# Attention values times the first matrix: from four matmuls with zero blocks to eight without, on one core

## The chip, the cores and the metric

The kernel runs on one core of one Trainium2 chip. The metric is device time in microseconds (us) of one launch, the median of several runs. Engines are named as in the profile: PE (TensorE) with its weight loads (PEld), DVE (VectorE), ACT (ScalarE), POOL (GpSimd), SP (SyncE, which issues the DMAs).

## What is computed

```python
def sm_attn(qq, kk, vv):                       # softmax attention, scale 1/8
    s = scale * np.matmul(qq, kk.transpose(0, 1, 3, 2))
    a = np.exp(s - np.max(s, axis=-1, keepdims=True))
    return np.matmul(a / (np.sum(a, axis=-1, keepdims=True) + 1e-09), vv)

# q, k, v: 4 batches x 8 heads x 576 x 64; p: 4 x 8 x 32 x 64
p_packed = sm_attn(p, k, v)                    # 32 rows of 64 per head
out = sm_attn(q, p_packed, p_packed)
x = out.transpose(0, 2, 1, 3).reshape(2304, 512)

h = x @ w_in                                   # first layers, d_ff 2048
x = (h * np.clip(h + 3.0, 0.0, 6.0) / 6.0) @ w_out

P = routing(x @ w_gate)                        # exp, then 8 rounds of row and column scaling
for e in range(8):                             # second layers, 8 experts, 1024 wide
    out += P[:, e:e + 1] * (np.maximum(x @ w1[e], 0.0) @ w2[e])
```

All inputs are float32 but the weights of the first layers, `w_in` and `w_out`, which come as 64-bit floats and are decoded on the chip.

## The kernel before, in words

Nothing is emitted in the order of the source. The functions put operations, each with an engine, an estimated cost, the tiles it reads and writes (`reads`, `writes`, `fills`, `takes`) and a priority, into an `Order`; `Order.run` then plays a list scheduler: again and again it takes the operation that can start first by its estimates (ties by priority), gives it buffers, and emits it. So each engine's order is fixed before the launch, and a changed cost or a changed use of a buffer lays out the following work anew. `place` says how many buffers a tag has. PSUM tiles `ph` and `po` have two banks each to begin with and two more each from `second_phase` on, which comes when the attention is finished.

*Attention* (L494, eight units `u`, two per batch `b`; unit `j` of a batch has heads 4j to 4j + 3). A unit loads k, p (in units 0 and 1 only: `p_sb[0]` for unit 0 and `p_sb[1]` for the seven others, L519), q and v, in this order on SP. GpSimd copies a unit's 128 rows of `p` (4 heads x 32) twice side by side (`pd`, L543); a transpose and a mask (`maskb`, L574 to L584) make of it, for each of two pairs of heads `g`, a 128 x 64 block matrix `pt`. The scores and the values of the packed rows follow, and a second mask (`maskz`, L692) lays them out so that after a transpose `ppT[:, g, :]` (L708) is 128 x 64: rows are head in the pair (h) times 64, columns head times 32, and the two blocks off the diagonal are zero. The scores of the queries use it as a whole (L740). The results `ax` of the attention (`a2`) have 128 rows, 4 heads x 32, per unit.

*packed_weights* (L830). Since `out` of a head is a 576 x 32 matrix times the 32 x 64 packed values, the values are multiplied into the first matrix first: for a batch and a group of 256 columns of `w_in`, `pw` = values times `w1`, two units j of 128 rows x 256. That is four matmuls per group (L841), for j and g: 128 rows (h times 64) x 64 columns, 256 columns moving, all of a group into one `ph` bank of 128 x 512, j being the half of the bank. ACT then copies the bank to the high part `pwh`, rounded (L857), and DVE writes the rest into `pwl` (L862), both 512 wide. For the first six units of work (`TOGETHER`) a call has one group, after that two.

*layer1a, layer2a* (L878, L913). A block of 384 tokens goes through two groups at a time: four times layer 1 from `pw` and `ax` in three float32r products (L890 to L892) into a `ph` bank, which ACT (L903) and DVE (L908) read; then four times layer 2 with 12 matmuls each (L928 to L930) into a `po` bank, added to `acc` by DVE (L943).

*After that* the gate (L1115: four matmuls of 128 rows x 32 columns, each on its own 32 columns of the array), the routing, and the second layers (`layer1b`, L996 to L998, and `layer2b`, L1055 to L1057), which take three quarters of the time.

The tiles of the early stage, `hs`, `tmp` and the raw weights (`raw`, L392; decoding `m` and `m_early`, L348 to L373) are shared by all this.

## Time and profile before

| | us |
|---|---|
| median of 3 runs | 1955.41 |
| fastest and slowest run | 1952.35, 1956.96 |
| span of the profiled execution | 1952.2 |
| PE busy in it | 1915.1 (98%) |
| DVE busy | 1210.0 (62%) |
| ACT busy | 970.2 (50%) |
| POOL busy | 947.5 (49%) |

Engine names and lines (L841 is line 841 of the kernel) are those of the listing above. "out<-in" names the tile written and the tiles read. A float32 matmul shows as two records, a float32r matmul as one. The records of PE overlap, since a matmul is still draining when the next one starts; what a series of them costs is therefore read from the start of the first to the start of what comes next. The chain of work that ended last is followed back from the last instruction, at each step to what released it.

### The profile page before, as it was taken

How to read it: one execution, taken by the hardware profiler on the slowest of the kernel's cores; microseconds unless marked ns; L12 is line 12 of the kernel's file. 1: busy time of each engine (PE TensorE's matmuls, PEld its weight loads, DVE VectorE, ACT ScalarE, POOL GpSimd, SP SyncE). 2: the span in 40 equal slices, each digit the busy share in tenths (PEclk: the TensorE clock that was granted, in tenths of full speed). 3: DMA queues.
4: the chain of work that ended last, by engine and by line, in shares of the span. 5: the costliest groups of instructions: out<-in, count | busy, mean ns of one | idle time of the engine just before them, and what ended most of it. 6: DMA issues, size and time to landing. Idle time of an engine off the chain costs nothing.

```text
span 1952.2 us, 28194 instructions
## 1 busy us (share of the span) xinstructions
PE 1915.1 (98%) x10573; PEld 1735.2 (89%) x10573; DVE 1210.0 (62%) x1998; ACT 970.2 (50%) x2135; POOL 947.5 (49%) x987
## 2 busy tenths in 40 slices
PE   6999999999999999999999999999999999999998
PEld 4789999998899999999899999999999999999997
DVE  6996686447866676666755555555555555555554
ACT  6885674335455555555544443344444344443432
POOL 2444675236665666655634544435344343444431
PEclk9999999999999999999999999999999999999999
DMA  9931121001222222222310101111110111101102
GB/s 215 188 90 33 54 66 44 11 1 44 65 65 66 75 65 70 71 65 65 87 33 33 44 22 44 33 33 33 33 44 30 36 33 33 44 22 44 33 11 66
DMA packets 103546, 104.87 MB, mean 54 GB/s; under 512 B 42736, under 2 KB 78576, under 8 KB 103408
## 3 DMA queue, kind: packets, MB, share of 16 engines
q1 hardware_dynamic: 103408, 103.06, 19.4%
q8 instruction: 83, 1.36, 0.3%
q14 instruction: 55, 0.45, 0.1%
HBM read 98.32 MB, written 4.72 MB: 53 GB/s over the span
## 4 chain that ended last, share of the span: by engine, by line
PE 91%; DVE 5%; ACT 2%; DMA 1%; issue 1%; SPq 0%; POOL 0%; DVEq 0%; POOLq 0%; ACTq 0%
PE po L1055 13%; PE po L1056 13%; PE po L1057 13%; PE ph L996 12%; PE ph L998 12%; PE ph L997 12%; PE po L928 3%; PE po L930 3%; PE po L929 3%; PE ph L890 2%; PE ph L892 1%; PE ph L891 1%; PE ph L841 1%; DMA raw<-in_moe_w_out_dram 1%; DVE tmp L908 0%
## 5 line engine op out<-in xcount | busy, mean ns | idle before, releaser
L1079 DVE SCALAR_TENSOR_TENSOR acc<-po,Pr,acc 128x512 f32<-128x512 f32 x504 | 377.3, 750 | 287.2 <-PE po L1057 284.1
L433 POOL TENSOR_TENSOR hsl<-tmp,hsh 128x384 fp32r<-128x384 f32 x382 | 391.8, 1031 | 325.4 <-ACT hsh L428 272.4
L1055 PE MATMUL po<-w2h,hsh 128*128 128x512 f32 x1152 | 449.0, 390 | 0.0
L1056 PE MATMUL po<-w2l,hsh 128*128 128x512 f32 x1152 | 448.8, 390 | 0.0
L1057 PE MATMUL po<-w2h,hsl 128*128 128x512 f32 x1152 | 448.6, 389 | 0.0
L433 POOL TENSOR_TENSOR w1xl<-m,w1xh 128x256 fp32r<-128x256 f32 x152 | 111.5, 758 | 321.8 <-ACT w1xh L428 321.8
L1057 PEld LDWEIGHTS po<-w2h,hsl 128*128 128x128 f32 x1152 | 216.2, 188 | 45.3
L304 ACT ACTIVATE tmp<-ph 128x384 f32<-128x384 f32 x241 | 117.7, 489 | 274.8 <-PE ph L998 263.1
L1055 PEld LDWEIGHTS po<-w2h,hsh 128*128 128x128 f32 x1152 | 216.3, 188 | 41.8 <-DVE acc L1079 0.2
L1056 PEld LDWEIGHTS po<-w2l,hsh 128*128 128x128 f32 x1152 | 216.3, 188 | 41.5
L428 ACT ACTIVATE hsh<-tmp 128x384 fp32r<-128x384 f32 x480 | 242.4, 520 | 20.4 <-DVE tmp L908 12.6
L1010 DVE TENSOR_TENSOR tmp<-ph,tmp 128x384 f32<-128x384 f32 x288 | 159.8, 556 | 149.3 <-PE ph L998 129.7
L428 ACT ACTIVATE w2h<-raw 128x1024 fp32r<-128x1024 f32 x64 | 67.9, 1061 | 350.1 <-PE po L1057 338.1
L1018 ACT ACTIVATE tmp<-tmp 128x384 f32<-128x384 f32 x288 | 149.6, 520 | 87.2 <-DVE tmp L1010 82.8
L996 PE MATMUL ph<-ax,w1h 128*128 128x384 f32 x448 | 151.5, 338 | 3.3 <-DVE tmp L1010 3.3
L998 PE MATMUL ph<-ax,w1l 128*128 128x384 f32 x448 | 150.7, 336 | 0.0
L997 PE MATMUL ph<-ax,w1h 128*128 128x384 f32 x448 | 150.7, 336 | 0.0
L433 DVE TENSOR_TENSOR hsl<-tmp,hsh 128x384 fp32r<-128x384 f32 x98 | 105.6, 1078 | 42.0 <-ACT hsh L428 39.8
L433 POOL TENSOR_TENSOR w1l<-raw,w1h 128x512 fp32r<-128x512 f32 (+1 forms) x104 | 116.3, 1132 | 7.5 <-ACT w1h L428 6.8
L996 PE MATMUL ph<-xyh,w1h 128*128 128x384 f32 x320 | 108.3, 339 | 3.6 <-ACT tmp L304 3.6
L455 POOL TENSOR_TENSOR m<-raw 128x256 f32<-128x256 f32 x58 | 44.5, 770 | 138.7 <-DMA raw<-in_moe_w_dram 136.0
L998 PE MATMUL ph<-xyh,w1l 128*128 128x384 f32 x320 | 108.1, 338 | 0.0
(207 smaller groups left out, 4040.4 us busy)
## 6 DMA issues: line engine op xcount, KB each, us to landing
raw<-in_moe_w_dram SPq DMA_DIRECT2D x128, 512.0 KB, 3.5
raw<-in_moe_w_in_dram SPq DMA_DIRECT2D x16, 512.0 KB, 3.9
raw<-in_moe_w_out_dram SPq DMA_DIRECT2D x16, 512.0 KB, 3.6
k<-in_k_dram SPq DMA_DIRECT2D x32, 144.0 KB, 5.9
q<-in_q_dram SPq DMA_DIRECT2D x32, 144.0 KB, 4.5
v<-in_v_dram SPq DMA_DIRECT2D x8, 576.0 KB, 6.5
out_dram<-acc SPq DMA_DIRECT2D x36, 128.0 KB, 2.3
p<-in_p_dram SPq DMA_DIRECT2D x1, 224.0 KB, 5.7
```

The lines of the kernel that those rows point to most:

```text
L304: ("ACT", t_act(n, True), lambda: nc.scalar.activation(dst(), src(), AF.Copy)),
L428: t_act(n), lambda: nc.scalar.activation(dst(w.t[0]), src(), AF.Copy),
L433: lambda e: e.tensor_tensor(dst(w.t[1]), src(), as_f32(dst(w.t[0])), ALU.subtract),
L996: nc.tensor.matmul(out, wh[:, at + c, :], bh[:, c, :], start=first and c == 0, **on)
L997: nc.tensor.matmul(out, wh[:, at + c, :], bl[:, c, :], start=False, **on)
L998: nc.tensor.matmul(out, wl[:, at + c, :], bh[:, c, :], start=False, **on)
L1010: t_dve(n), lambda: nc.vector.tensor_tensor(u.t, ps.t[:, :n], u.t, ALU.add),
L1018: t_act(n, bool(ps)), lambda: nc.scalar.activation(c.t, src(), AF.Relu),
L1055: nc.tensor.matmul(ps.t, hh[:, f, ts], wh[:, f, :], start=(f == 0), stop=False)
L1056: nc.tensor.matmul(ps.t, hh[:, f, ts], wl[:, f, :], start=False, stop=False)
L1057: nc.tensor.matmul(ps.t, hl[:, f, ts], wh[:, f, :], start=False, stop=(f == NFC - 1))
L1079: lambda row=row, share=share, ps=ps: nc.vector.scalar_tensor_tensor(row(), ps.t, share(), row(), ALU.mult, ALU.add),
```

## The change

Each group's product of values and first matrix is split in two again, by head: the zero blocks of `ppT` are no longer multiplied. A matmul takes 64 rows (one head's 64) and the 32 columns of that head. To give the two units of a batch different places in the array, the heads of each second unit are swapped in pairs: unit j = 1 has its heads in the order 1, 0, 3, 2 within each 32-row block, in `p` (loaded in four pieces), in both masks (three blocks wide, of which a unit takes two, from j on) and so in all that follows. A call writes two `ph` banks, one for each j, with the groups side by side in each; ACT and DVE take them out in pieces of 256.

```diff
-        if u < 2:
-            of = slice(0, 1) if u == 0 else slice(1, NU)
+        if u in (0, 2):
+            of = slice(0, 1) if u == 0 else slice(1, B)
             dma(
                 64 * (of.stop - of.start),
                 lambda: nc.sync.dma_start(
-                    p_sb[u].t, p.rearrange("b (j h) n d -> (h n) (b j) d", j=2)[:, of, :]
+                    p_sb[u].t, p.rearrange("b (j h) n d -> (h n) j b d", j=2)[:, 0, of, :]
                 ),
                 writes=[p_sb[u]], **kw,
             )
+        if u == 1:
+            for x in range(4):
+                dma(
+                    32,
+                    lambda x=x: nc.sync.dma_start(
+                        p_sb[u].t[32 * x:32 * x + 32],
+                        p[:, 4 + (x ^ 1)].rearrange("b n d -> n b d"),
+                    ),
+                    fills=[p_sb[u]], **kw,
+                )
+        p_of = p_sb[1] if j else p_sb[min(u, 2)]
+        p_at = b if j else max(b - 1, 0)
...
-        gps(
+        turns["pd"] = [gps(
             0.55,
             lambda: nc.gpsimd.tensor_copy(
-                pd.t, p_sb[min(u, 1)].t[:, max(u - 1, 0), None, :].to_broadcast([128, 2, D])
+                pd.t, p_of.t[:, p_at, None, :].to_broadcast([128, 2, D])
             ),
-            reads=[p_sb[min(u, 1)]], writes=[pd], **kw,
-        )
+            reads=[p_of], writes=[pd], after=turns["pd"], **kw,
+        )]
...
-                maskb.rearrange("p h n -> p (h n)")[:, None, :].to_broadcast([128, 2, 2 * NP]),
+                maskb[:, j:j + 2].rearrange("p h n -> p (h n)")[:, None, :].to_broadcast([128, 2, 2 * NP]),
...
-                maskz.rearrange("p g h d -> p g (h d)"),
+                maskz[:, :, j:j + 2].rearrange("p g h d -> p g (h d)"),
...
-        pss, got = [psum("ph") for _ in w1s], [pair("pw", [128, 2, FG]) for _ in w1s]
+        banks, got = [psum("ph") for _ in range(2)], [pair("pw", [128, 2, FG]) for _ in w1s]
 
         def mm():
-            for ps, w1 in zip(pss, w1s):
-                for j in range(2):
-                    for g in range(2):
-                        nc.tensor.matmul(
-                            ps.t[64 * g:64 * g + 64, j * FG:(j + 1) * FG],
-                            ppTs[2 * b + j].t[:, g, :],
-                            w1.t[:, 2 * j + g, :],
-                            start=True, stop=True,
-                        )
+            for x, w1 in enumerate(w1s):
+                for g in range(2):
+                    for j in range(2):
+                        for h in range(2):
+                            r0, n0 = 64 * h, 32 * (h ^ j)
+                            nc.tensor.matmul(
+                                banks[j].t[64 * g + n0:64 * g + n0 + 32, x * FG:(x + 1) * FG],
+                                ppTs[2 * b + j].t[r0:r0 + 64, g, n0:n0 + 32],
+                                w1.t[r0:r0 + 64, 2 * j + g, :],
+                                start=True, stop=True,
+                            )
...
-                0.6 * len(w1s) + 0.4, mm, reads=[ppTs[2 * b], ppTs[2 * b + 1], *w1s], writes=pss, takes=got,
+                0.45 * len(w1s) + 0.2, mm, reads=[ppTs[2 * b], ppTs[2 * b + 1], *w1s], writes=banks, takes=got,
...
-        for ps, w in zip(pss, got):
-            high = act(
-                t_act(2 * FG, True), lambda ps=ps, w=w: nc.scalar.activation(flat(w.t[0]), ps.t, AF.Copy),
-                reads=[ps], fills=[w], **quick,
-            )
+        for x, w in enumerate(got):
+            for j in range(2):
+                src = lambda x=x, j=j: banks[j].t[:, x * FG:(x + 1) * FG]
+                high = act(
+                    t_act(FG, True),
+                    lambda src=src, w=w, j=j: nc.scalar.activation(w.t[0][:, j], src(), AF.Copy),
+                    reads=[banks[j]], fills=[w], **quick,
+                )
...
```

The DVE part of each piece follows in the same way. `p_sb` becomes three tiles: `p0` for unit 0, `p1` for the second units of all four batches, `p2` for the first units of batches 1 to 3.

## Rows read from the trace of the kernel before

**Rows 1.** The page, chain that ended last: shares by engine, then by line.
```profile
PE 91%; DVE 5%; ACT 2%; DMA 1%; issue 1%; SPq 0%; POOL 0%; DVEq 0%; POOLq 0%; ACTq 0%
PE po L1055 13%; PE po L1056 13%; PE po L1057 13%; PE ph L996 12%; PE ph L998 12%; PE ph L997 12%; PE po L928 3%; PE po L930 3%; PE po L929 3%; PE ph L890 2%; PE ph L892 1%; PE ph L891 1%; PE ph L841 1%; DMA raw<-in_moe_w_out_dram 1%; DVE tmp L908 0%
```
**Rows 2.** The chain by stretch: 0 to 130, to 257.5, to 307, to 455 us.
```profile
by line: DMA raw<-in_moe_w_out_dram 8.2%; DVE m_early L348 6.8%; issue 3.5%; DVE tmp L908 3.5%; PE tp L683 3.4%; PE tp L599 3.3%; DMA q<-in_q_dram 3.1%; DVE m_early L364 2.9%; PE tp L740 2.8%; SPq L510 2.6%; PE tp L647 2.5%; PE po L928 2.3%
by line: PE po L928 19.9%; PE po L930 19.8%; PE po L929 19.8%; PE ph L890 11.2%; PE ph L892 10.0%; PE ph L891 10.0%; PE ph L841 9.0%; DVE tmp L908 0.4%; issue 0.1%
by line: DVE m L348 17.1%; DVE tmp L908 8.8%; DVE hsl L433 8.0%; POOL m L348 7.8%; issue 7.2%; DVE m L367 7.1%; DVE m L364 5.2%; DVE acc L943 5.2%; DVE m L373 4.8%; DVE pwl L862 4.8%; ACT m L371 4.6%; DVE m L455 4.0%; DVE w1l L433 2.9%; ACT
by line: PE po L928 19.1%; PE po L930 19.0%; PE po L929 19.0%; PE ph L890 10.2%; PE ph L892 9.1%; PE ph L891 9.1%; PE ph L841 5.8%; PE ph L1115 3.2%; PE ph L996 1.6%; PE ph L998 1.4%; PE ph L997 1.4%; PE ph L1125 1.3%; DVE tmp L908 0.3%; is
```
**Rows 3.** Stages: length, busy us (records) of PE, PEld, DVE, ACT, POOL; clock, DMA, GB/s.
```profile
0.00:130.00 130.00, 107.07 (x1070) 87.05 (x1070) 109.12 (x287) 100.12 (x252) 50.57 (x54) 1.00 0.83 175
130.00:257.50 127.50, 127.21 (x803) 120.03 (x801) 88.39 (x161) 83.16 (x197) 73.21 (x84) 1.00 0.16 48
257.50:307.00 49.50, 48.11 (x298) 44.13 (x297) 45.64 (x88) 35.56 (x89) 38.08 (x45) 1.00 0.22 65
```
**Rows 4.** Line 841 alone: records, ns least/median/most, first and last start, shape.
```profile
L841 PE MATMUL ph<-w1f,ppT x256: 379/379/431, 38.5 to 397.8; 128*64 128x256 f32 x128
```
**Rows 5.** The chain in order of time, first short and long call: start, us, what.
```profile
140.25 1.01 PE ph L841 x8
159.61 1.88 PE ph L841 x16
```
**Rows 6.** PE in order of time at a gate: start, us, line, tiles, shape.
```profile
375.42 0.85 PE L1115 MATMUL ph<-acc,wg 128*32 128x384 f32 x8
376.20 0.36 PE L890 MATMUL ph<-ax,pwh 128*128 128x192 f32 x1
```
**Rows 7.** Lines 857, 304, 862, 908: ACT and DVE instructions that read PSUM.
```profile
L857 ACT ACTIVATE pwh<-ph x32: 577/588/616, 40.6 to 400.8; 128x512 fp32r<-128x512 f32 x32
L304 ACT ACTIVATE tmp<-ph x241: 469/492/496, 376.5 to 1934.7; 128x384 f32<-128x384 f32 x121
L862 DVE TENSOR_TENSOR pwl<-ph,pwh x32: 674/680/697, 41.8 to 401.4; 128x512 fp32r<-128x512 f32 x32
L908 DVE SCALAR_TENSOR_TENSOR tmp<-tmp,ph x96: 537/553/556, 49.2 to 439.6; 128x384 f32<-128x384 f32 x96
```
**Rows 8.** PE in order of time, second halves of two long calls; idle before.
```profile
290.83 1.08 PE L841 MATMUL ph<-w1f,ppT 128*64 128x256 f32 x8 [0.27 <-DVE tmp L908]
307.07 1.08 PE L841 MATMUL ph<-w1f,ppT 128*64 128x256 f32 x8 [0.94 <-DVE tmp L908]
```
**Rows 9.** PE behind a long call: first records of layers 1, 2 and 1.
```profile
161.42 0.44 PE L890 MATMUL ph<-ax,pwh 128*128 128x384 f32 x1
...
162.57 0.34 PE L928 MATMUL po<-hsh,w2h 128*128 128x384 f32 x1
...
170.99 0.33 PE L890 MATMUL ph<-ax,pwh 128*128 128x384 f32 x1
```
**Rows 10.** SP's issues of DMAs in order of time, units 0 and 1.
```profile
5.22 0.98 SPq L519 DMA_DIRECT2D p<-in_p_dram  x1
...
17.14 1.41 SPq L519 DMA_DIRECT2D p<-in_p_dram  x1
18.64 3.17 SPq L527 DMA_DIRECT2D q<-in_q_dram  x4
...
22.76 1.41 SPq L510 DMA_DIRECT2D k<-in_k_dram  x2
27.86 0.35 SPq L392 DMA_DIRECT2D raw<-in_moe_w_out_dram  x1
```
**Rows 11.** The page, DMA issues: count, KB each, median us to landing.
```profile
q<-in_q_dram SPq DMA_DIRECT2D x32, 144.0 KB, 4.5
```
**Rows 12.** PE in order of time: first transposes of unit 1's q.
```profile
27.73 0.60 PE L647 MATMUL tp<-ident,q 128*128 128x128 f32 x4
```

More of the change, by code (lines that the diff above doesn't have):

```diff
@@ L262, in tile_kernel @@
     ones = const.tile([128, 128], F32, name="ones")
-    maskb = const.tile([128, 2, NP], F32, name="maskb")
-    maskz = const.tile([128, 2, 2, D], F32, name="maskz")
+    maskb = const.tile([128, 3, NP], F32, name="maskb")
+    maskz = const.tile([128, 2, 3, D], F32, name="maskz")
     three = const.tile([128, 1], F32, name="three")
@@ L821, in tile_kernel @@
     fin = [hold(f"acc{j}", [128, TB // 128, DM]) for j in range(NB)]
-    chain, turns = {}, {"pw": [], "l1": []}
+    chain, turns = {}, {"pd": [], "pw": [], "l1": []}
     def psum(tag):
@@ L853, in packed_weights @@
         ]
-        flat = lambda t: t.rearrange("p j f -> p (j f)")
-        for ps, w in zip(pss, got):
-            high = act(
-                t_act(2 * FG, True), lambda ps=ps, w=w: nc.scalar.activation(flat(w.t[0]), ps.t, AF.Copy),
-                reads=[ps], fills=[w], **quick,
-            )
-            dve(
-                t_dve(2 * FG),
-                lambda ps=ps, w=w: nc.vector.tensor_tensor(
-                    flat(w.t[1]), ps.t, as_f32(flat(w.t[0])), ALU.subtract
-                ),
-                reads=[ps], fills=[w], after=[high], **quick,
-            )
+        for x, w in enumerate(got):
[6 more added lines that the diff above has]
+                )
+                dve(
+                    t_dve(FG),
+                    lambda src=src, w=w, j=j: nc.vector.tensor_tensor(
+                        w.t[1][:, j], src(), as_f32(w.t[0][:, j]), ALU.subtract
+                    ),
+                    reads=[banks[j]], fills=[w], after=[high], **quick,
+                )
         return got
@@ L1215, in tile_kernel @@
         nc.vector.memset(maskb, 0.0)
-        nc.vector.memset(maskb[0:64, 0, :], 1.0)
+        nc.vector.memset(maskb[0:64, 0:3:2, :], 1.0)
         nc.vector.memset(maskb[64:128, 1, :], 1.0)
@@ L1221, in tile_kernel @@
                 r0 = 64 * g + 32 * h
-                nc.vector.memset(maskz[r0:r0 + 32, g, h, :], 1.0)
+                nc.vector.memset(maskz[r0:r0 + 32, g, h:3:2, :], 1.0)
         place("p0", att, 1)
         place("p1", att, 1)
-        p_sb = hold("p0", [128, 1, D]), hold("p1", [128, NU - 1, D])
+        place("p2", att, 1)
+        p_sb = hold("p0", [128, 1, D]), hold("p1", [128, B, D]), hold("p2", [128, B - 1, D])
         for u in range(NU):
```

## Prediction

> **What bounds the kernel now.** I read the chain of work that ended last first, for the whole span and then by stretch, because the change lies in one stage of several. Over the whole span the chain is 91% TensorE, and half of that is the two matmul lines of the last layers, which the diff doesn't touch; line 841, the line it rewrites, is 1% of it [rows 1]. By stretch [rows 2] the picture splits into four. Up to 130 us the chain hops between DMA, VectorE, ScalarE and TensorE: the attention units and the early weights. From 130 to 257.5 us it is TensorE almost alone, and line 841 is 9.0% of it. From 257.5 to 307 us it runs through VectorE: the decoding of weights (L348 to L373) and the results of layer 1 queue there. From 307 us on it is TensorE again, 5.8% of it line 841 up to 455 us. The busy times say the same [rows 3]: TensorE 127.21 of 127.5 us in the second stretch, VectorE 45.64 of 49.5 in the third; the granted clock is 1.00 in them, the upper level of 2.4 GHz. So a microsecond off line 841 is a microsecond off the end in the second and fourth stretch, doubtful in the first, and worth nothing in the third unless VectorE also gets shorter.
>
> **What line 841 costs.** 256 records are 128 matmuls of two records each, 128 rows x 64 columns against 256 moving columns [rows 4]. There are 20 calls: 8 for one group (8 records, 1.01 us from the first start to the next line's) and 12 for two groups (16 records, 1.88 us) [rows 5]. The second group's 8 records cost 1.88 - 1.01 = 0.87 us, so two records on the two column halves share a slot of 0.87 / 4 = 0.2175 us, and 0.14 us per call is fixed. That records on different columns really run together, and are not merely short, is seen at the gate: four matmuls of 32 columns and 384 moving columns, 8 records, take 376.20 - 375.42 = 0.78 us [rows 6]. A slot scaled to 384 columns is 0.326 us; two at a time would be 4 slots, 1.31 us, and one matmul after the other with only the neighbours' records overlapping would be 5 slots, 1.63 us. Four at a time is 2 slots, 0.65, plus 0.14: 0.79, which is what stands there. So column strips run side by side, both records of a matmul on one strip one after the other, and a later matmul doesn't wait for the second record of an earlier one.
>
> **The change, the matmuls.** A group's 4 matmuls become 8 of 64 rows x 32 columns, each at its own place in the array: two row halves, four column strips, none used twice. The streamed length is the same, 256. No row of this trace shows two row halves at work together, so the price of a call is bounded from both sides. If all eight run together, a group is 2 slots instead of 4: a call for two groups takes 0.14 + 4 x 0.2175 = 1.01 us (saves 0.87), a call for one 0.575 us (saves 0.435). If row halves take turns, four strips at a time as at the gate, it is 16 records / 4 = 4 slots a group, as now, and nothing is saved. I take the first end: strips that share no part of the array were independent at the gate, and the swap of heads gives every matmul a place of its own and the two halves of a strip different banks. The Trainium skill, page "TensorEngine Tiling (Array Packing)", section "Restrictions and Gotchas", speaks against it: it says that different row tiles cannot access the same PSUM bank simultaneously, and here each bank is written by both row halves, in different partitions. No run here shows it yet; by that rule the saving would be zero.
>
> **The change, where the saving counts.** All 20 calls at full price would give 12 x 0.87 + 8 x 0.435 = 13.9 us. The chain's shares place the calls: 9.0% of 127.5 us is 11.5, five long and two short ones; 5.8% of 148 is 8.6, four long and the second half of one more [rows 2, 5]. So five long calls start in the second stretch, four after 307 us, three in the VectorE stretch. There TensorE already stands before the second half of line 841 until VectorE has read an older bank, 0.27 and 0.94 us [rows 8], and a shorter call only lengthens that. Of the eight short calls six start before 130 us and two in the second stretch. Counted: 9 x 0.87 + 2 x 0.435 = 8.7 us. The six early ones I count at nothing; if their 2.6 us came through too it would be better by that.
>
> **The change, what it adds.** The results of a call leave the banks in pieces of 256 instead of 512. ScalarE took 588 ns for 512 and 492 ns for 384 [rows 7], so about 396 for 256 and 2 x 396 - 588 = 204 ns more per pair; VectorE 680 for 512 and 553 for 384, so about 426, and 2 x 426 - 680 = 172 ns more. 32 pairs: 6.5 us on ScalarE, 5.5 us on VectorE. Where TensorE leads, both have room (88.4 and 83.2 of 127.5 us busy [rows 3]) and the cost is nothing; the cover is TensorE's own work behind the call, one piece of layer 1 and then 8.4 us of layer 2 that needs no `ph` bank [rows 9]. Without that cover it would be some 0.4 us a call. In the VectorE stretch it is on the path: 3 calls x 2 x 0.17 = 1.0 us. In the first stretch, with six short calls, it is 6 x 0.37 = 2.2 us if both engines carry the chain all the time; they and TensorE share it, and I take half, 1.1.
> The load of `p` becomes six DMAs instead of two, with the same bytes. SyncE was in the issue of the 32 KB one 0.98 us and of the 224 KB one 1.41 us [rows 10]. Four pieces for unit 1 are about 3.9 us, 2.5 more, and they are queued ahead of unit 1's q loads; one more is in unit 2. Behind them SyncE has 3.7 us to spare before the next weight load at 27.86, which waits for its buffer, so that doesn't move. The q loads do: issued by 21.8 us and landing 4.5 us later [rows 11], at 26.3, they would land at 28.8 against the first q transpose at 27.73 [rows 12]. That is 1.1 us at most and nothing at least, since TensorE has gaps there; I take 0.5.
> The new order among the `pd` copies on GpSimd keeps the order that stood, and a copy that waits there holds up only weight decoding; wider masks are set once in the prologue, while the first loads are on their way. I count both at nothing; the loads cover them, and uncovered they would be some tenths of a microsecond.
> A call for one group now takes both `ph` banks. Before 130 us there are only two, and layer 1 needs them; that is a rival below, and nothing in the sum, because TensorE has attention work of the next units to fill with.
>
> **The sum.** -8.7 + 1.0 + 1.1 + 0.5 = -6.1 us. The profiled span is 1952.2 us, 3.2 under the median of 1955.41 and beside the fastest of the three runs (1952.35); so the span becomes 1946.1 and the median 1949.3. The planner gets new costs and lays out the first 450 us anew; what this does to the VectorE stretch no row tells, and I allow 3 us either way, twice what TensorE stands idle there (49.5 - 48.11 = 1.4 [rows 3]).
>
> **Rivals.**
> (B) Each column strip works its records in program order. Then the second record of the upper half's matmul blocks the lower half's first, and halves overlap by one record only: 3 slots for a group, 5 for two. A long call saves 3 x 0.2175 = 0.65, a short one 0.22; 9 x 0.65 + 2 x 0.22 = 6.3, less the same 2.6: -3.7, 1951.7 us. For it: two records of one strip are never seen side by side here. Against it: the gate's strips overtake each other's second records. The Trainium skill, page "TensorE: Matmul & The Clock Gate", section "Part 3: Packing small matmuls", says that matmuls start and end in strict program order; the 0.78 us of the gate fit that only if the two records of its four matmuls are interleaved in the stream, which no view here tells.
> (C) Row halves take turns. Nothing saved, 2.6 us of additions: 1958.0 us.
> (D) Slower: the two `ph` banks of the first stretch. A short call has to find both empty, and holds both until four pieces each on ScalarE and VectorE are through, so layer 1 loses a turn at each of the six calls. A lost turn puts one piece of layer 1 (1.15 us) and its quarter of layer 2 (8.42 / 4 = 2.1 us) behind 130 us, where TensorE has no gap: 3.25 us each [rows 9], 19.5 for six. With the savings kept that is -6.1 + 19.5, 1968.8 us; it decides from about three lost turns on. For it: 23 us of TensorE's first 130 are idle [rows 3], so work put off there isn't made up later. Against it: turns are lost only if no layer 1 work could run in between anyway, and the attention sets the pace there.
> (E) Better: the early calls and the VectorE stretch give their share too, and the additions hide: -13.9, 1941.5 us.
>
> **How the numbers follow.** Forecast 0.47, B 0.19, C 0.16, D 0.12, E 0.06. What can be told from no change is 0.2%, 3.9 us: faster is under 1951.5, slower over 1959.3. The forecast with its 3 us is faster at four fifths, else the same; B is split down the middle; C is the same, at times slower; D nearly always slower; E faster. Together 0.54 faster, 0.30 same, 0.16 slower. For 8 in 10 the range runs from 1942 (between E and the forecast's low edge) to 1960 (past C, short of most of D).
>
> **What would show it.** In the changed profile a long call should be 32 records in about 1.01 us and a short one 16 in about 0.58; 1.23 and 0.79 would be B, 1.9 and 1.0 C. The stretch between 130 and 257 us should be shorter by about 5 us, the one led by VectorE not at all; the pieces of 256 should read near 396 and 426 ns; the six short calls should leave as many pieces of layer 1 before 130 us as now, and fewer would be D. The forecast is wrong if the calls keep their length, or if TensorE's waits for VectorE grow by more than 3 us.

## The result, and the profile after

| | before | after |
|---|---|---|
| median, us | 1954.99 | 1972.98 |
| fastest and slowest run | 1952.35, 1956.96 | 1966.33, 1975.3 |
| span of the profiled execution | 1952.2 | 1973.5 |
| ratio of the times (95% interval) | | 1.0089 (1.0069 to 1.0109) |

The change makes the kernel 18 us slower. The forecast was 6 us faster, with a range that ended at 1960. The new matmuls do what was forecast; the time goes in other places. A trace shows one execution: that of after is the slowest of its four and that of before the fastest, so that the spans lie 21.3 us apart and the medians 18.0; after's four runs go with the granted clock, from 1966.33 us at a mean of 0.997 to 1975.3 at 0.991. First the part that came true: the records of the new line, one long call in the chain, a short call in PE's order of time, and ACT's and DVE's pieces.

```profile
L855 PE MATMUL ph<-w1f,ppT x512: 373/376/633, 41.7 to 410.5; 64*32 64x256 f32 x171
```
```profile
174.51 1.02 PE ph L855 x32
```
```profile
45.14 0.66 PE L855 MATMUL ph<-w1f,ppT 64*32 64x256 f32 x16
45.74 0.33 PE L659 MATMUL tp<-ident,q 128*128 128x128 f32 x1
```
```profile
L873 ACT ACTIVATE pwh<-ph x64: 362/378/409, 42.4 to 413.9; 128x256 fp32r<-128x256 f32 x64
L878 DVE TENSOR_TENSOR pwl<-ph,pwh x64: 407/415/426, 43.1 to 414.9; 128x256 fp32r<-128x256 f32 x64
```

A long call takes 1.02 us (forecast 1.01, before 1.88 [rows 5]), a short one 0.60 (forecast 0.575, before 1.01). The pieces read 378 and 415 ns (forecast 396 and 426). By the lengths of the calls 20 of them save 13.6 us. Now the stages, in the columns of [rows 3]:

```profile
0.00:130.00 130.00, 104.41 (x1008) 84.06 (x1009) 102.77 (x273) 94.23 (x242) 44.27 (x47) 0.92 0.84 170
130.00:257.50 127.50, 124.23 (x917) 115.20 (x916) 83.68 (x169) 80.93 (x200) 70.56 (x78) 0.99 0.15 50
257.50:307.00 49.50, 46.64 (x343) 42.70 (x342) 42.89 (x84) 36.34 (x95) 39.62 (x48) 0.97 0.21 65
307.00:455.00 148.00, 145.52 (x1020) 136.46 (x1019) 78.12 (x143) 63.29 (x144) 62.82 (x65) 1.00 0.06 19
```

Up to 130 us PE does less than before (104.41 us busy, before 107.07), at a granted clock of 0.92 where it was 1.00. In the second stretch, where it hardly stood before, it now stands 3.3 us. And the stage of the second layers, which the diff doesn't touch, got longer. Its own line shows that: starts of the first and the last of the 1152 matmuls, for before, after and the first two experiments that matter for it.

```profile
L1055 PE MATMUL po<-w2h,hsh x1152: 389/389/500, 458.9 to 1946.1; 128*128 128x512 f32 x192
```
```profile
L1071 PE MATMUL po<-w2h,hsh x1152: 387/389/495, 471.7 to 1967.2; 128*128 128x512 f32 x192
```
```profile
L1056 PE MATMUL po<-w2h,hsh x1152: 387/389/497, 461.6 to 1956.7; 128*128 128x512 f32 x192
```
```profile
L1065 PE MATMUL po<-w2h,hsh x1152: 389/389/499, 464.2 to 1949.5; 128*128 128x512 f32 x192
```

This view is the ruler for all that follows. The first start is the loss up to there: 471.7 - 458.9 = 12.8 us. The distance to the last start is the pace behind it: 1487.2 us before, 1495.5 after, 8.3 more. Together 21.1, of the 21.3 between the two spans. In the table each ratio is to runs of before made beside it on the same chip; the ruler's two columns are of one execution each, so that a difference of 2 us between them says little unless the medians have it too.

The last two columns are how many us the granted clock was 0.50, the level of 1.2 GHz, before the first start and in the distance behind it. While the clock is 0.50, PE loses at most half of the time (an estimate from the two levels; 24 matmuls shown below took 2.39 us at 0.50 and 1.53 at 1.00). By this estimate after's 27 us are worth up to 13.6.

| run | median, us | ratio (95% interval) | first start | distance | 0.50 before | 0.50 behind |
|---|---|---|---|---|---|---|
| before | 1954.99 | | 458.9 | 1487.2 | 0 | 7 |
| after | 1972.98 | 1.0089 (1.0069 to 1.0109) | 471.7 | 1495.5 | 27 | 7 |
| e1, 640 B unused | 1963.13 | 1.0038 (1.0025 to 1.0051) | 461.6 | 1495.1 | 3 | 7 |
| e2, swap, old matmuls | 1969.38 | 1.0068 (1.0051 to 1.0084) | 468.8 | 1493.4 | 17 | 3 |
| e3, p as before | 1968.14 | 1.0066 (1.0050 to 1.0082) | 463.3 | 1493.3 | 10 | 3 |
| e4, e3, late tiles in place | 1959.06 | 1.0025 (1.0016 to 1.0034) | 464.2 | 1485.3 | 3 | 3 |
| e5, e4, short calls old | 1960.05 | 1.0031 (1.0018 to 1.0043) | 466.3 | 1487.3 | 14 | 7 |
| e6, e5, bank by bank | 1961.54 | 1.0037 (1.0024 to 1.0051) | 464.7 | 1487.6 | 3 | 7 |
| e7, before, small matmuls, no swap | 1958.3 (one run) | | 463.2 | 1487.2 | 0 | 7 |
| e8, e5, five banks | 1959.49 | 1.0025 (1.0013 to 1.0037) | 462.3 | 1487.7 | 10 | 0 |
| e9, before, swap at the masks | 1954.86 | 1.0000 (0.9991 to 1.0009) | 459.6 | 1487.2 | 0 | 7 |
| e10, e9, long calls new, five banks | 1952.57 | 0.9987 (0.9978 to 0.9997) | 456.2 | 1488.7 | 0 | 3 |
| **e11**, e10, old costs in the plan | **1949.73** | 0.9973 (0.9964 to 0.9983) | 455.6 | 1486.4 | 0 | 0 |
| e12, before, five banks | 1953.70 | 0.9995 (0.9986 to 1.0005) | 458.2 | 1488.7 | 0 | 3 |
| e13, e11, p in pieces | 1960.85 | 1.0026 (1.0017 to 1.0036) | 462.7 | 1488.3 | 10 | 3 |
| e14, e11, short calls new | 1957.89 | 1.0017 (1.0007 to 1.0027) | 462.3 | 1486.6 | 3 | 0 |
| e15, e11, four banks | 1953.51 | 0.9994 (0.9984 to 1.0003) | 459.2 | 1485.7 | 7 | 3 |
| e16, before, attention tiles moved | 1957.03 | 1.0012 (1.0003 to 1.0022) | 461.5 | 1485.4 | 3 | 3 |

The distances hold stretches at 0.50 too. With half of these taken off, they fall into three groups (an estimate from the table): 1484 us with the late tiles where before has them and four banks each for `ph` and `po`, 1486 to 1488 with five and three (e8, e10 to e14), 1492 with the longer pool described next. So the kernels with five and three banks pay some 3 us in the second layers, whatever the long calls are.

### The profile page after: what moved, and what is told of

It is laid out like the page before. It is cut to its first block, busy times and chain, and to the rows that moved or that the text cites. A ratio compares the mean times of both kernels' runs of the same rounds, so it can differ in the third digit from the quotient of the medians.

```text
span 1973.5 us, 28804 instructions
## 1 busy us (share of the span) xinstructions
PE 1926.5 (98%) x10829; PEld 1743.7 (88%) x10829; DVE 1208.5 (61%) x2021; ACT 973.6 (49%) x2170; POOL 950.4 (48%) x993
## 4 chain that ended last, share of the span: by engine, by line
PE 87%; DVE 6%; ACT 3%; DMA 2%; issue 1%; POOL 1%; SPq 0%; DVEq 0%; POOLq 0%; ACTq 0%
PE po L1071 13%; PE po L1072 13%; PE po L1073 13%; PE ph L1012 12%; PE ph L1014 12%; PE ph L1013 12%; PE po L944 2%; PE po L946 2%; PE po L945 2%; PE ph L906 1%; PE ph L907 1%; PE ph L908 1%; DMA raw<-in_moe_w_out_dram 1%; DMA k<-in_k_dram 1%; PE ph L855 1%
## 5 line engine op out<-in xcount | busy, mean ns | idle before, releaser
L433 DVE TENSOR_TENSOR hsl<-tmp,hsh 128x384 fp32r<-128x384 f32 x102 | 110.0, 1078 | 42.1 <-ACT hsh L428 37.5
L1013 PE MATMUL ph<-xyl,w1h 128*128 128x384 f32 x320 | 108.5, 339 | 0.0
L1012 PE MATMUL ph<-ax,w1xh 128*128 128x384 f32 x320 | 108.5, 339 | 0.0
```

The source lines that it names most:

```text
L433: lambda e: e.tensor_tensor(dst(w.t[1]), src(), as_f32(dst(w.t[0])), ALU.subtract),
L1012: nc.tensor.matmul(out, wh[:, at + c, :], bh[:, c, :], start=first and c == 0, **on)
L1013: nc.tensor.matmul(out, wh[:, at + c, :], bl[:, c, :], start=False, **on)
```

## The experiments

**The place of the tiles.** The wider masks make the pool of constants 640 B longer in each partition (128 for `maskb`, 512 for `maskz`), and what lies above it moves up by as much: `raw`, `acc`, `hs`, `w1h`, `w2h`. e1 is before with nothing but such a gap.

```diff
     maskz = const.tile([128, 2, 2, D], F32, name="maskz")
+    const.tile([128, 160], F32, name="gap0")
```

> The kernel before with one unused tile of 640 bytes per partition behind its constants, so that all that lies behind them (weights, results, work tiles) moves by 640 bytes, as in the changed kernel. Theory 'place': the 8.5 us that the changed kernel loses slowly between 450 us and the end come from where the tiles lie; then this kernel is slower by about 8 us (1963) and its float32r matmuls of 384 columns in the second layers follow each other at 175 to 176 ns instead of 173. Rival: the slow loss is of the chip or the run; then 1955 and 173 ns.

Measured: 1963.13, 8 us slower with not one instruction changed, and the distance of the ruler is 1495.1. All four runs with the longer pool (after, e1, e2, e3) have 1493.3 to 1495.5 there, the fourteen others 1485.3 to 1488.7. The place costs about 8 us behind 455 us. Of the 2.7 us in e1 before that, 3 us at 0.50 are worth up to 1.7. The trace shows which matmuls pay: those of 384 columns (`layer1b`). Two starts with sixteen steps between them, of before and of e1, are 2.77 and 2.83 us apart, 173 and 177 ns a step; those of 512 columns (`layer2b`) begin 227 ns apart in both (median).

```profile
708.92 0.34 PE L996 MATMUL ph<-ax,w1h 128*128 128x384 f32 x1
711.69 0.34 PE L997 MATMUL ph<-ax,w1h 128*128 128x384 f32 x1
```
```profile
712.53 0.34 PE L997 MATMUL ph<-ax,w1h 128*128 128x384 f32 x1
715.36 0.34 PE L998 MATMUL ph<-ax,w1h 128*128 128x384 f32 x1
```

Which tile's place it is, and why, these runs don't tell.

**The swap with its load, without the new matmuls.** e2 is after with the old line 841, its cost in the plan and its full-width pieces.

> Of the change only the swapped heads (p in four pieces and a fifth for the first units, masks of three blocks, the order of the pd copies); line 841 and its banks as before. Theory 'load': the loss of the first 130 us comes from the pieces of p ahead of unit 1's q, TensorE stands and the granted clock falls; then the loss stands here without the shorter calls to pay for it: 12.7 + about 9 = 22 us by 450 us, with the slow loss about 1980 to 1985. Rival 'banks': the loss comes from short calls that take both ph banks; then this kernel is near 1955, or 1963 with the slow loss.

Measured: 1969.38. Against e1 (same places) it is 468.8 - 461.6 = 7.2 us later at the ruler's start, with 17 us at 0.50 where e1 has 3. So most of the loss up to there comes without a single new matmul.

**p loaded as before.** e3 is after with `p` in two loads; the order of heads is swapped where `maskb` is applied, by two half-width instructions in units with j = 1.

```diff
-                maskb[:, j:j + 2].rearrange("p h n -> p (h n)")[:, None, :].to_broadcast([128, 2, 2 * NP]),
+            parts_of = [(slice(0, 64), slice(0, 64), maskb[:, 0:2])] if j == 0 else [
+                (slice(NP * c, NP * c + NP), slice(NP * (1 - c), NP * (1 - c) + NP), maskb[:, 1 + c:2 + c])
+                for c in range(2)
+            ]
```

> The changed kernel, but p is loaded as before in two DMAs and in the order of its heads; the swap is made where the transposed p is masked, by two VectorE instructions of half the width in the second units. Theory 'load': the first 130 us are as before, the calls of line 855 keep 1.02 and 0.59 us, so about 1948, and with the slow loss 1956. Rival 'banks': the early loss stays, about 1973.

Measured: 1968.14, first start 463.3, 8.4 before after's (in the medians 4.8). What goes wrong stands in after's trace, SP first, then PE, then the granted clock, to be held against [rows 10] and [rows 12]:

```profile
17.70 2.90 SPq L528 DMA_DIRECT2D p<-in_p_dram  x4
20.70 1.92 SPq L539 DMA_DIRECT2D q<-in_q_dram  x3
25.65 0.36 SPq L392 DMA_DIRECT2D raw<-in_moe_w_out_dram  x1
26.05 0.54 SPq L539 DMA_DIRECT2D q<-in_q_dram  x1
```
```profile
25.91 0.33 PE L586 MATMUL tp<-ident,pd 128*128 128x128 f32 x1 [0.74 <-POOL pd L555]
28.09 2.19 PE L611 MATMUL tp<-kT,pt 128*64 128x288 f32 x8 [1.85 <-DVE pt L591]
32.28 2.18 PE L659 MATMUL tp<-ident,q 128*128 128x128 f32 x9 [0.75 <-DVE ax L825]
35.86 2.39 PE L695 MATMUL tp<-v,a1T 96*64 96x128 f32 x24
```
```profile
10.00:26.00 16.00, 11.46 (x105) 7.79 (x105) 10.96 (x25) 9.50 (x25) 2.98 (x4) 1.00 1.00 194
27.40:37.60 10.20, 8.64 (x44) 6.30 (x46) 7.98 (x23) 6.42 (x17) 1.87 (x3) 0.50 1.01 241
51.30:58.10 6.80, 6.80 (x44) 5.83 (x43) 1.34 (x3) 4.26 (x10) 1.27 (x1) 0.50 0.92 208
```

The four pieces took SP 2.90 us, 1.5 more than the one load before. But the scheduler wrote a new order: the load of weights that before came after the next unit's k now stands between the third and the fourth q, and it waits for its buffer until 25.65. Unit 1's mask waits on DVE behind a softmax of unit 0, PE stands 0.74 and 1.85 us, and its q transposes begin at 32.28 in place of 27.73. With that comes the second loss: the granted clock is 0.50, the level of 1.2 GHz, from 27.4 to 37.6 and from 51.3 to 58.1 us, and the 24 matmuls of L695 take 2.39 us, where before took 1.53:

```profile
32.51 1.53 PE L683 MATMUL tp<-v,a1T 96*64 96x128 f32 x24
```

Before reads 1.00 in [rows 3] throughout; its first stretch at 0.50 comes at 526.6 us. By the estimate above the clock is the larger part: after has 17 us more at 0.50 than e3, worth up to 8.5, and e2 14 us more than e1, worth up to 6.8.

**The same with the late tiles in place.** In e4 the two masks lie in the attention's own pool, a gap of their old size stays, and the late tiles are where before has them.

```diff
-    maskb = const.tile([128, 3, NP], F32, name="maskb")
-    maskz = const.tile([128, 2, 3, D], F32, name="maskz")
+    const.tile([128, 320], F32, name="gap0")
+    maskb = att.tile([128, 3, NP], F32, name="maskb")
+    maskz = att.tile([128, 2, 3, D], F32, name="maskz")
```

> As the kernel before it in this list (p loaded as before, eight small matmuls), and the masks moved out of the constants into the attention's own pool with an unused tile in their place, so that weights and work tiles of the later layers lie where they lay before. Theory 'load' with 'place': about 1948, 173 ns between the matmuls of 384 columns. If 'place' is wrong, the same as without the move.

Measured: 1959.06, and the distance is 1485.3 again. Still, with all new matmuls and neither of the two faults, it was slower than before. Three runs sought the rest in the calls. e5 keeps the short calls in the old form, e6 writes a long call bank by bank (j outermost), e8 gives `ph` five banks in the late stage and `po` three, in place of four each.

```diff
-    place("ph", ph, 2, 2)
-    place("po", ph, 2, 2)
+    place("ph", ph, 2, 3)
+    place("po", ph, 2, 1)
```

> As e4 (p loaded as before, swap at the mask, places of the later tiles as before), and the eight short calls as in the kernel before: four matmuls, one ph bank, results in pieces of 512. Only the twelve long calls have the eight small matmuls. Theory 'banks': the 4.7 us that e4 loses between 135 and 157 us are short calls and layer 1 waiting for the two ph banks of that stage; then they are gone, the stage is as before, and the long calls give 12 x 0.86 = 10.3 less the waits of 6 to 8 us that e4 shows beside them: 1950 to 1952. Rival 'order': the loss there is of the planner's new order, whatever the banks; then as e4, 1959.

> As e5, but a long call does all matmuls into its first bank before those into the second, and its results are read bank by bank. Theory 'banks': the second bank is asked for half a call later, so that the waits inside long calls shrink by up to 0.5 us each where they stand, 1 to 3 us in all (1948 to 1950). Of the array: if matmuls overtake each other however far apart in the order, an undisturbed long call stays at 1.02 us; if they overtake only their neighbours, it is 1.9 us (four places at a time) and the kernel is near 1960.

> As e5, with five ph and three po banks from the second phase on instead of four and four. Theory 'banks': the waits of long calls for a second bank are gone where VectorE isn't the pace, 3 to 4 us less than e5 (1947). If VectorE sets the pace at every one of these waits, nothing changes against e5; if the second layers need their fourth po bank, it is slower than e5.

Measured: 1960.05, 1961.54, 1959.49. None of the three explains it; e5 was even later at the start of the ruler (466.3), with 14 us at 0.50. The order within a call matters little: bank by bank it takes 1.05 us. e7 asked whether the swap is needed at all: before, with eight small matmuls but unswapped heads, so that two matmuls of a group share each place in the array.

> The kernel before (heads in their order, p, masks and places of tiles as before) with the changed calls, eight matmuls of 64 rows x 32 columns, but without the swap: both units of a batch use the same four places of the array, so two matmuls share a place. If a place is what has to be free, a group is 4 slots and a long call stays at 1.88 us, a short one at 1.01; if only banks or rows count, they are 1.02 and 0.59. The time: 1.88 us gives 1955 plus what banks and pieces of 256 cost, 1957 to 1965.

```profile
160.77 1.89 PE ph L843 x32
```

A long call has its old length, 1.89 us. It is the swap that makes the gain.

**Nothing moved.** e9 to e12 move no tile at all: masks of the old size at the old place, `p` as before, and the swap by two half-width DVE instructions at both masks in the four units with j = 1, with unchanged costs in the plan. e9 has the old calls; e10 the new long calls (short ones old) and five late `ph` banks; e11 the same with the planner told the old cost; e12 is before with the five banks alone. (Where expectations speak of one bank left for the others, or of a third pair, it is this one bank that changes hands; `po` keeps three.)

```diff
-                maskz.rearrange("p g h d -> p g (h d)"),
+            parts_of = [(slice(0, 128), maskz.rearrange("p g h d -> p g (h d)"))] if j == 0 else [
+                (slice(D * h, D * h + D), maskz[:, :, 1 - h, :]) for h in range(2)
+            ]
...
-                0.45 * len(w1s) + 0.2, mm, reads=[ppTs[2 * b], ppTs[2 * b + 1], *w1s], writes=banks, takes=got,
+                0.6 * len(w1s) + 0.4, mm, reads=[ppTs[2 * b], ppTs[2 * b + 1], *w1s], writes=banks, takes=got,
```

> Before, with the heads of each second unit swapped, but p loaded as before, the two masks of their old size at their old place, the swap made by two half-width VectorE instructions in place of one at each of the two masks (16 instructions in all, some 0.1 us each, 0.8 us), old matmuls, old plan: no tile moves. If the early loss of the runs with natural p came from the swap itself (two instructions for one), this run loses it too: +3 to +5 us, 1957 to 1959. If it came from tiles of the attention stage that moved by 1792 B, or from the new matmuls, this run is as before within 1.5 us: 1953 to 1956.

> The run above, with the long calls in the new form (64 rows x 32 columns, two banks by unit) and five late banks for them, one for the other matmuls; short calls in the old form. Against the run with five banks and masks in the attention pool (1959.5, lost 9 us by 160 us, then gained 5) only the place of the tiles differs. If the early loss was the place of the attention stage's tiles: the profile stands within 2 us of before at 160 us and ends 4 to 6 us under it, 1948 to 1951, and both kernels are beaten. If it came with the new plan or the new matmuls themselves: +6 to +9 us at 160 us again, and 1957 to 1960.

> The same with the planner told the old cost of a call (1.6 in place of 1.1 for a long one), so that the written order is nearly that of before. If the early loss is the order that the planner writes for shorter calls, it goes here and not in the run above: 1948 to 1951 here against 1957 to 1960 there. If it is the place of tiles, both gain alike, within 2 us of each other. If the matmuls themselves cost the neighbouring work, both lose alike.

> Before with five late banks for these calls and one for the other matmuls, nothing else: the control for the two runs above. If the drains of the banks are what the long calls wait for in the VectorE-paced stretch, a third pair of banks gives up to 1.3 us (rows of before: 0.94 and 0.27 us of waits for it): 1953 to 1955. If the single bank left for the others is short, slower by 1 to 3 us: 1956 to 1958. In neither case does it explain a gain of 4 us in the runs above.

Measured: 1954.86, 1952.57, 1949.73, 1953.70. The swap done this way costs nothing that can be told. e11 beats both kernels: 0.9973 (0.9964 to 0.9983), 5 us under before, and the fifth bank by itself (e12) isn't told from nothing. Between e8 and e10 lie 6.9 us, though they differ only in where masks and attention tiles lie, in how the second mask is applied, and by 0.065 us for the first one in the plan. The 0.065 us are enough for another order: e8 does eight of unit 1's transposes of q in one go, e10 puts another transpose of a `pd` ahead of them, as before does.

```profile
27.32 1.09 PE L653 MATMUL tp<-ident,q 128*128 128x128 f32 x8
```
```profile
27.62 0.33 PE L574 MATMUL tp<-ident,pd 128*128 128x128 f32 x1
```

By 44 us the two orders have parted on every engine. The place doesn't do it: e3 and e4, and before and e16 below, have the same order on VectorE, ScalarE, GpSimd and SyncE although their tiles lie apart. So e3 to e6 and e8, all with these 0.065 us, were compared with before under another order; e8 has 10 us at 0.50, e10 none. The plan's costs of the long calls (e10 to e11) are worth 2.8 us. The line of e11 and its stages:

```profile
L888 PE MATMUL ph<-w1f,ppT x384: 376/376/402, 160.9 to 393.3; 64*32 64x256 f32 x192
```
```profile
0.00:130.00 130.00, 106.74 (x1065) 86.79 (x1065) 107.53 (x291) 98.78 (x250) 48.81 (x52) 1.00 0.82 173
130.00:257.50 127.50, 125.64 (x893) 118.27 (x890) 89.86 (x174) 83.95 (x208) 73.98 (x84) 1.00 0.16 50
257.50:307.00 49.50, 45.62 (x351) 42.21 (x349) 43.35 (x88) 35.73 (x94) 36.56 (x44) 1.00 0.21 65
```
```profile
303.65 1.09 PE L888 MATMUL ph<-w1f,ppT 64*32 64x256 f32 x32
306.98 0.44 PE L939 MATMUL ph<-ax,pwh 128*128 128x384 f32 x1 [2.24 <-DVE tmp L957]
```

The first stretch is that of before (1065 records of 1070, clock 1.00). In the third, led by VectorE, PE stands more than it did (45.62 busy of 49.5, before 48.11): a call is through in 1.02 us, and what follows it waits 2.24 us for DVE to read a bank; before, the second half of the call waited 0.94 for it [rows 8]. What this does to the saving, the starts of the first and the ninth long call show, the ninth being the first behind the VectorE stretch. Before's first is in [rows 5], its ninth comes first here, then both of e11:

```profile
334.68 1.95 PE L841 MATMUL ph<-w1f,ppT 128*64 128x256 f32 x16
```
```profile
160.89 1.09 PE L888 MATMUL ph<-w1f,ppT 64*32 64x256 f32 x32
334.69 1.09 PE L888 MATMUL ph<-w1f,ppT 64*32 64x256 f32 x32
```

From first to ninth before takes 175.1 us and e11 173.8: eight calls, each 0.86 us shorter, gain 1.3. From the ninth to the ruler's start before takes 124.2 and e11 120.9: four calls gain 3.3 of the 3.4 that their lengths promise. Between first and ninth PE is busy 5.5 us less in e11 and stands 4.1 us more. The waits for DVE's reads grow from 1.2 to 2.2 us; those of layer 2 for GpSimd's low part of its input, `hsl`, grow more, e11 first:

```profile
PE po L978 <- POOL hsl L433: 3.2, 7, 0.9
```
```profile
PE po L929 <- POOL hsl L433: 0.2, 1, 0.2
```

**One part added to e11 at a time.** e13 loads `p` in pieces as the change does, with its three `p` tiles and its fixed order of the `pd` copies (no late tile moves, the masks pick blocks accordingly), e14 takes the new form for the short calls too, e15 has four late banks. e16 is before with its attention tiles 1920 B higher, as e4, e5, e6 and e8 have them (1920 B, not the 1792 B of an expectation above).

> The run that beat both kernels (1949.7), with p loaded as in the change: unit 1's heads swapped by four transfers of 32 partitions, two more loads for the first units, the copies of p kept in order; the masks pick the blocks accordingly, no late tile and no tile of the attention stage except p's own moves. If the four transfers delay unit 1 and the stage behind it, as the two runs with and without them say (7 to 8 us by 455 us), then 1956 to 1959, with stretches at half clock in the first 100 us. If that difference came from the masks' place or from the longer const pool, it stays at 1949 to 1952.

> The run that beat both kernels, with the eight short calls in the new form too (two banks by unit, pieces of 256 columns for ScalarE and VectorE), same costs told to the planner. By their array time (1.01 to 0.59 us, eight calls) they give up to 3.4 us: 1946.4. If a short call now waits for two free banks in place of one while the attention stage holds them, or VectorE's shorter pieces cost more there, that gain is lost: 1949 to 1953.

> The run that beat both kernels, with four banks for these calls and two for the others, as before and after have them. If a long call that needs both banks at its start stands for the drain of the call before it, the wait that lay beside its first half comes into the open: one to three waits of 1 to 4 us, 1952 to 1956. If the two pairs are enough, 1949 to 1951.

> Before with the two masks in the attention stage's pool and a gap of their size in their old place: the tiles of the attention stage lie 1920 B higher, over other late tiles than before; late tiles, instructions and their costs for the planner are as before. If the early loss of 5 to 9 us of the runs built that way came from this place (which late tile waits for which early one), before loses it too: 1959 to 1963, and the difference stands by 160 us. If it came from the new matmuls in that layout, before is unmoved: 1953.5 to 1956.

Measured: 1960.85, 1957.89, 1953.51, 1957.03. The pieces of `p`, with the order of the copies, cost e11 7.1 us at the ruler's start (462.7 against 455.6), as 7.2 and 8.4 in the two comparisons before. Of these, 10 us at 0.50 are worth up to 5, and e11 has none. (The rest of e13's trace reads 0.95, at the pace of the other runs with five banks.) SP's order is that of after:

```profile
17.58 2.79 SPq L528 DMA_DIRECT2D p<-in_p_dram  x4
20.47 1.92 SPq L539 DMA_DIRECT2D q<-in_q_dram  x3
25.74 0.36 SPq L392 DMA_DIRECT2D raw<-in_moe_w_out_dram  x1
26.14 0.54 SPq L539 DMA_DIRECT2D q<-in_q_dram  x1
```

The short calls, 0.4 us shorter each, cost 6.7 us there (8.2 in the medians). The order is another one here too, from 43 us on. The fifth call shows how, in PE's order of time:

```profile
130.22 0.34 PE L905 MATMUL ph<-ax,pwl 128*128 128x384 f32 x1
131.59 0.62 PE L852 MATMUL ph<-w1f,ppT 64*32 64x256 f32 x4 [1.04 <-DVE tmp L921]
132.78 0.65 PE L852 MATMUL ph<-w1f,ppT 64*32 64x256 f32 x12 [0.56 <-DVE tmp L921]
134.91 0.63 PE L807 MATMUL tp<-ident,e 128*128 128x128 f32 x4 [1.48 <-DVE e L798]
```

It waits for one bank, then for the other, and the attention's transposes behind it come late; behind these waits the clock is 0.50 for 3 us. Before, the fifth call ran at 99.9 us and took one bank, in e11 at 101.1. Four late banks in place of five cost e11 3.6 us at the start. The order is that of e11 up to 390 us. The wait for DVE's read of a bank now stands behind a call of the second stretch too, where before had none, and in the VectorE stretch inside a call, ahead of its second bank; behind this wait the clock is 0.50 for 7 us, worth up to 3.4:

```profile
245.39 1.09 PE L888 MATMUL ph<-w1f,ppT 64*32 64x256 f32 x32
247.25 0.44 PE L939 MATMUL ph<-ax,pwh 128*128 128x384 f32 x1 [0.77 <-DVE tmp L957]
```
```profile
307.38 1.95 PE L888 MATMUL ph<-w1f,ppT 64*32 64x256 f32 x28 [2.68 <-DVE tmp L957]
337.85 1.09 PE L888 MATMUL ph<-w1f,ppT 64*32 64x256 f32 x32
```
```profile
306.80:313.60 6.80, 6.21 (x41) 4.92 (x42) 6.14 (x10) 3.46 (x10) 5.61 (x6) 0.50 0.23 77
```

The ninth call, in the last PE line, comes 3.2 us after e11's.

The moved attention tiles cost before 2.6 us (461.5 against 458.9, and 2.6 in the medians), in the same order. Of these, 3 us at 0.50 are worth up to 1.7. The clock falls behind a wait for k of 1.42 us; before, at the same place, waited 1.56 us and kept its clock:

```profile
35.60 0.69 PE L557 MATMUL tp<-ident,k 96*128 96x96 f32 x6 [1.56 <-DMA k<-in_k_dram]
```
```profile
35.45 1.07 PE L558 MATMUL tp<-ident,k 96*128 96x96 f32 x6 [1.42 <-DMA k<-in_k_dram]
```
```profile
35.60:39.00 3.40, 3.40 (x34) 2.58 (x35) 0.79 (x2) 1.68 (x5) 0.00 (x0) 0.50 1.08 218
```

Part of what e4, e5, e6 and e8 lost may be the place that I had given the masks, but by itself it isn't the 6.9 us between e8 and e10.

## Why the prediction was wrong

The sum said -6.1 us, and 18.0 more were measured. By their size, the steps that failed are the wider masks, of which it says "I count both at nothing" (8 us); the loads behind `p`, with "so that doesn't move" (7 to 8); the short calls (6.7); and the price of the long calls in the second stretch (2 in e11, 5 in e15). One by one:

- *Length of the calls*: right. 1.02 and 0.60 us; B (1.23, 0.79) and C (1.88, 1.01) are out. The Trainium skill, page "TensorEngine Tiling (Array Packing)", section "Restrictions and Gotchas", says that different row tiles can't access one PSUM bank at the same time. The 1.02 us differ from that: each bank was written by both row halves, in different partitions. The Trainium skill, page "TensorE: Matmul & The Clock Gate", section "Part 3: Packing small matmuls", has matmuls start in strict program order. Bank by bank (e6) the second unit's matmuls would then start two slots late, which makes 6 slots or 1.45 us; 1.05 was measured, so the trace differs here too.
- *Where the saving counts*: wrong in part. 8.7 us were counted. The four calls after 307 us gave 3.3 of their 3.5 in e11. The step that failed is "a microsecond off line 841 is a microsecond off the end" for the second stretch. Its five calls were to give 4.35 us, with 1.0 lost behind them; from the first long call to the ninth only 1.3 of the 175.1 us came off in e11, and 177.2 were taken in e15. What the calls save there PE spends on other engines: in e11 3.2 us in waits for GpSimd (before 0.2) and 2.2 for DVE's read of a bank (before 1.2); in e15, where a call needs its second bank sooner than the old one did and there are only four, 1.4 and 4.1. In all, twelve new long calls gave 1 us with four banks (e15, an interval that holds zero) and 5 with five (e11), nothing else moved.
- *Short calls*: wrong sign. Counted as 0.9 us gained; in e14 they lose 6.7 at the ruler's start. Rival D had the place, two banks in the first stretch, and by its mark one turn is lost: by 130 us e14 has started 32 records of the first layer 1 line against 34, two to a piece. By D's price that is 3.25 us; the rest is the wait of the call itself, of the attention behind it, and the clock. (After has 26, but e2 with the old calls 28: three of its four lost turns go with `p`.)
- *Pieces of 256*: right, 378 and 415 ns.
- *p in pieces*: the delay of q was named, its size and way were not. Forecast 0.5, at most 1.1 us; measured 7 to 8 us by the start of the second layers (in the medians 5 between after and e3, 11 between e13 and e11). SP's issue time was smaller than estimated (2.9 us against 3.9). What failed is "Behind them SyncE has 3.7 us to spare before the next weight load at 27.86, which waits for its buffer, so that doesn't move": the order on the queue is written by the scheduler, and with more loads it was another one, with a load that waits for a buffer ahead of the fourth q. The half clock was in no step, and it can be the larger part. Pieces and the order of the copies were not tried apart.
- *Wider masks*: wrong. Counted at nothing, because their instructions cost nothing. Their 640 B cost 8 us in the stage that holds three quarters of the time (e1). No rival had it.
- *The new plan, 3 us either way*: held between e10 and e11 (2.8 us), not between e8 and e10, where 0.065 us in the plan and the place of some tiles made 6.9.
- *Readings*: the last layers are 75 of the chain's 91% in [rows 1], six lines and not "half of that"; and the two alternatives for the gate, 1.31 and 1.63 us, leave out the fixed 0.14. Neither changes the forecast.

The parts don't add up by themselves: place 10.6 (e1, both columns of the ruler), `p` 7 to 8, short calls 6.7, less the 1 us that the long calls give with four banks, is more than the 21.1 measured. That `p` and the short calls work on the same first 160 us and in part replace each other is argued, not shown; and the time at 0.50, which enters each of these differences, follows from none of them alone. What stays open is why a 640 B shift slows matmuls of 384 columns, which of two like waits drops the clock, and whether a call could do with one bank per group; the last was not tried, since the two row halves of one column strip would then write the same partitions of a bank at once.

## What to carry to other kernels

Price what a change does to the order and to the places of the things around it, not only its own instructions: more small loads on a queue, or some hundred bytes in a pool that lies below everything, can cost more than the edit can gain. A shorter matmul call pays only as far as the banks that it needs are free when it starts, so count the banks with the array time. Read the granted clock by stretch in every run that you compare: here 10 us at 0.50 hold up to 5 us that would else be put down to the edit. And undo the parts one by one: here the core of the change was worth 5 us, with one bank more for it, once everything else was left where it was.

## What the runs showed of the hardware

- Eight float32 matmuls of 64 rows x 32 columns on eight different places run all together: 16 records in 0.60 us, 32 in 1.02, and 1.05 written bank by bank; with two of them on one place 1.89.
- The place of tiles in a partition changes the pace of matmuls: 640 B further up, those of 384 columns began 176 ns apart (median) in place of 173, and the second layers took 1495 us in place of 1487, every instruction the same.
- In after the granted clock fell to 0.50 at 27.4 us, in the second of two waits of 0.74 and 1.85 us, and stayed there for 10 us while PE worked 8.64 of them. Twelve of the eighteen traces have such stretches before the second layers, every time in or behind waits of PE; but a wait of 1.42 us in e16 was followed by one, and a wait of 1.56 us at the same place in before was not.
